# A two-layer block replanned: phi of the keys on GpSimd, query weights turned by DMA, MLP blocks of four tiles, last product in halves

## The chip, the core and the metric

The kernel runs on one core of one Trainium2 chip. The metric is the device time of one execution in microseconds (us). The engines are PE (TensorE, with PEld for its weight loads), DVE (VectorE), ACT (ScalarE), POOL (GpSimd) and SP, which here only issues DMAs. All runs quoted carry the state "fast".

## The reference, cut to what matters

The input has 2048 tokens (16 tiles of 128) of width 512, in bf16. Attention, then MLP, each with a residual; then both once more with the same weights.

```python
x = x + A(layernorm(x)); x = x + B(layernorm(x)); x = x + A(layernorm(x)); x = x + B(layernorm(x))

def A(x):                      # linear attention, 32 heads of 16
    q, k, v = heads(x @ wqkv)
    pq, pk = q @ w_phi, k @ w_phi
    phi_q = concat(softmax(pq), softmax(-pq)); phi_k = concat(softmax(pk), softmax(-pk))
    kv, z = phi_k^T @ v, sum(phi_k)          # over all 2048 tokens
    return ((phi_q @ kv) / (phi_q . z + 1e-6)) @ wo

def B(x):                      # gated MLP, inner width 1376
    return (relu(x @ W_gate) * (x @ W_up)) @ W_down
```

The sum over all tokens matters: no tile can be attended before the last tile's keys have been summed. From the start to that point ("the key phase") each tile is normalized and turned, multiplied by key and value weights, pushed through exp, divided by its row sums ("phi") and summed into `kv`. The query and key weights are first multiplied by `w_phi` ("the fold"), for which they have to be turned.

## The kernel before

The kernel writes all operations down with costs and priorities, lets a small planner of its own simulate them, and then issues them in the planned order. The order on each engine is thereby fixed; semaphores do the rest. The planner knows that some DVE instructions and POOL exclude each other (`port`).

```python
POOL_PHI = (1930, 1940)        # ns: occupies, latency
XPOSE = (1200, 2430)           # a DMA transpose
RATE = 265.0                   # bytes per ns for loads

def plan(ops):
    # ...
    for o in cand:
        t = max(clock[e], o.ready, port if o.port else 0.0, lanes[0] if o.move else 0.0)
    # ... the earliest goes next
    if o.port:
        port = t + occ
```

A tile's normalization in layer A runs on DVE and takes the port; so does phi on either engine:

```python
n = op("DVE", SCALE, due, lambda: nc.vector.tensor_scalar(
    out=xn.t[:], in0=x_of(t), scalar1=mv[:, t, 0:1], scalar2=rs[:, t:t + 1], op0=Alu.subtract,
    op1=Alu.mult), [a], [xn], name="xnA", port=True)
# ... in Keys.tile, after exp (ek), row sums (sk) and their reciprocals:
if phi_eng == "POOL":
    a = [op("POOL", POOL_PHI, due, lambda: phi(nc.gpsimd, 0, 2), [a], [ph], [ek, sk], name="phi", port=True)]
# ...
else:   # "BOTH": half on DVE, half on POOL; before, all 16 tiles of the first layer
    a = [op("DVE", dve(512), due, lambda: phi(nc.vector, 0, 1), [a], [ph], [ek, sk], name="phi", port=True),
         op("POOL", (965, 975), due, lambda: phi(nc.gpsimd, 1, 1), [a], (), [ek, sk, ph], name="phi", port=True)]
```

The MLP works on blocks of one or two tiles:

```python
BLOCKS = ((1, 1, 2, 2, 2, 2, 2, 2, 2), (1, 1, 2, 2, 2, 2, 2, 2, 1, 1))
# ... in mlp(l, t0, n, ...), with W = n * P columns:
for q, (g, m) in enumerate(fs):
    for b in range(NB):
        nc.tensor.matmul(ps.t[:m, q * W:(q + 1) * W], lhsT=w[:, b, g * P:g * P + m],
                         rhs=xT.t[:, b, 0:W], start=(b == 0), stop=(b == NB - 1))
```

The softmax here doesn't subtract the row's maximum and nothing guards it: scores larger than these inputs give would overflow.

Of the kernel before, what the change touches and what calls it, by code (L numbers as in the profile page):

```python
# [8 lines left out]
P = 128  # L9
# [227 lines left out]
XPOSE = (1200, 2430)  # L237
RATE = 265.0
# [16 lines left out]
BLOCKS = ((1, 1, 2, 2, 2, 2, 2, 2, 2), (1, 1, 2, 2, 2, 2, 2, 2, 1, 1))  # L255
# [3 lines left out]
def kernel(  # L259
# [25 lines left out]
    wk, wv, wq, wo = (new(n, [NB, D]) for n in ("wk", "wv", "wq", "wo"))  # L285
# [15 lines left out]
    p_wT = pool("wT", 1, [NB, D])  # L301
# [7 lines left out]
    p_xB = pool("xnTB", 3, [NB, 2 * P], fifo=True)  # L309
    p_h = pool("hT", 2, [NF * 2 * P], fifo=True)  # L310
# [15 lines left out]
    wqkv = A_wqkv.rearrange("(b p) f -> p b f", p=P)  # L326
    x_in = [None] * T
    x_in[0] = load(0, X[0][:, 0, :], xv[:, 0, :], 131072)
    l_wk = [load(0, wk[:, b:b + 2, :], wqkv[:, b:b + 2, D:2 * D], 262144, "ACT") for b in (0, 2)]
    l_wf = load(1, wf[:], A_w_phi.rearrange("(b j) d f -> (j d) b f", b=NB, j=8), 65536)  # L330
    x_in[1] = load(2, X[0][:, 1, :], xv[:, 1, :], 131072)
    l_wv = load(3, wv[:], wqkv[:, :, 2 * D:3 * D], 524288, "ACT")
    op("ACT", (1300, 1300), 5, lambda: nc.scalar.preload_act_table_set("natural_log_exp_and_others"), name="tbl")
    wov = A_wo.rearrange("(h bb c) f -> c h bb f", bb=NB, c=C)
    gv, uv = (w.rearrange("(b p) f -> p b f", p=P) for w in (B_W_gate, B_W_up))
    dv = B_W_down[0:10 * P, :].rearrange("(f p) d -> p f d", p=P)
    l_wq, l_wo, l_wg, l_wu, l_wd = [], [], [], [], []
    late = [("q", wq[:, b, :], wqkv[:, b, 0:D], 131072) for b in range(NB)]
    late += [("g", wg[:, b, :], gv[:, b, :], 352256) for b in range(NB)]
    late += [("o", wo[i * H:(i + 1) * H, :, :], wov[i], 131072) for i in range(C)]  # L340
    late += [("u", wu[:, b, :], uv[:, b, :], 352256) for b in range(NB)]
    late += [("d", wd[:, f:f + 2, :], dv[:, f:f + 2, :], 262144) for f in range(0, 10, 2)]
    late += [("d", wd[:96, 10, :], B_W_down[10 * P:F, :], 98304)]
    homes = dict(q=l_wq, g=l_wg, o=l_wo, u=l_wu, d=l_wd)

    def load_next(after, due):
        if late:
            kind, dst, src, nbytes = late.pop(0)
            homes[kind].append(load(due, dst, src, nbytes, follow=[after]))
# [29 lines left out]
    def fold(w, dst, loaded, due, step, engs):  # L379
        wT = Buf(p_wT)  # L380
        turned, done = [], []
        for m in range(NB):
            ps = Buf(p_b)
# [6 lines left out]
        for m in range(NB):  # L390
# [3 lines left out]
                start=True, stop=True) for b in range(NB)], [turned[m], c_blk] + turned[:m], [ps], [wT], name="fold")  # L394
# [7 lines left out]
    def turn(src, dst, how, due, after, takes, uses, name):  # L402
        if how == "SP":
            return op("SP", XPOSE, due, lambda: nc.sync.dma_start_transpose(out=dst(), in_=src.t[:]), [after],
                      takes, [src] + uses, name=name, move=500)
# [13 lines left out]
    def norm_A(l, t, due, after, how):  # L419
# [11 lines left out]
        return turn(xn, lambda: xnTA[c][:, :, i * P:(i + 1) * P], how, due, n, [], [], "xnTA")  # L431


    class Keys:
# [6 lines left out]
        def tile(self, t, due, due_v, due_z, xT, phi_eng, v_eng="ACT"):  # L441
# [12 lines left out]
                for b in range(NB)], [xT, l_wv], [vp], name="V")  # L454
# [119 lines left out]
    def mlp(l, t0, n, due_x, due_g, due_d, after, how):  # L574
# [3 lines left out]
        turned = []  # L578
        for i in range(n):
            t = t0 + i  # L580
            a = stats(l, "B", t, due_x(i), [after[t]])
            xc = Buf(p_xn)
# [6 lines left out]
            out=tmp[:, t0:t0 + n], in0=mv[:, t0:t0 + n, 1], scalar1=EPS, scalar2=None, op0=Alu.add), [a], name="ve")  # L589
# [44 lines left out]
        for i in range(n):  # L634
            t = t0 + i
            yp = Buf(p_b)
            last = None
            for lo, hi in ((0, 4), (4, 8), (8, NF)):
# [18 lines left out]
    for t in range(T):  # L657
        if t == 2:
            x_in[2] = load(4, X[0][:, 2, :], xv[:, 2, :], 131072)
            x_in[3] = load(5, X[0][:, 3, :], xv[:, 3, :], 131072)  # L660
# [86 lines left out]
```

## Time and profile before

| | before |
|---|---|
| median of the first 3 runs | 402.99 us |
| span of the profiled execution | 401.2 us |
| PE busy | 387.8 us (97%) |
| DVE, ACT, POOL busy | 275.5, 259.5, 22.1 us |

The top of the page and the engines' line, before. Busy PE is not PE at its peak: the record of a matmul of 512 columns is 0.379 us long, but the next one can start 0.216 us after it.

```profile
span 401.2 us, 8365 instructions
PE 387.8 (97%) x3176; PEld 265.9 (66%) x3176; DVE 275.5 (69%) x685; ACT 259.5 (65%) x704; POOL 22.1 (6%) x24
```

The table of stretches, before. Columns: the stretch in us, its length, then busy us (and instructions) of each engine, granted clock, share of DMA engines, GB/s.

```profile
core 0: us, PE busy (x) PEld busy (x) DVE busy (x) ACT busy (x) POOL busy (x), PEclk, DMA share, GB/s
10.00:40.00 30.00, 26.06 (x188) 14.02 (x188) 29.81 (x58) 25.20 (x78) 9.01 (x8) 1.00 0.60 138
40.00:62.00 22.00, 21.72 (x154) 12.09 (x155) 19.54 (x30) 20.63 (x59) 9.44 (x9) 1.00 0.62 174
62.00:80.00 18.00, 16.69 (x171) 11.38 (x170) 15.08 (x52) 18.00 (x60) 0.00 (x0) 1.00 0.13 23
80.00:250.00 170.00, 169.72 (x1326) 117.07 (x1324) 121.07 (x276) 106.69 (x283) 2.99 (x2) 1.00 0.16 31
```

From 80 to 250 us PE is full. From 10 to 40 us DVE is full (29.81 of 30) and PE is not. From 62 to 80 us ACT is full: the first attended tiles wait for one another's results there.

The chain of waits, before: start, length, what.

```profile
36.10 4.13 DMA xnTA<-xn
...
137.49 9.61 PE b L607 x88
...
397.08 0.75 DVE X L648
397.83 0.66 DVEq L742
```

88 gate and up matmuls of 256 columns take 9.61 us, 0.109 us each. A transposed tile took 4.13 us to land at 36.1 us. The kernel ends with a residual of 0.75 us on DVE and a store.

Phi and the normalizations of the first layer, before, from the views of these two tiles; the three durations are min/median/max in ns.

```profile
L466 POOL TENSOR_TENSOR phiK<-ek,sk x16: 1054/1056/1717, 16.5 to 58.9; 128x512 bf16<-128x512 bf16 x16
L466 DVE TENSOR_TENSOR phiK<-ek,sk x16: 652/692/1358, 17.9 to 58.8; 128x512 bf16<-128x512 bf16 x16
...
L427 DVE TENSOR_SCALAR xn<-X,mvA,rsA x16: 390/403/1097, 8.7 to 45.8; 128x512 bf16<-128x512 bf16 x16
```

### The profile page before, as it was taken

The page shows a single profiled execution, that of the slowest core. Times are in us where ns is not written, and L with a number is a line of the kernel's source. Part 1 is how long each engine was busy: PE and PEld are TensorE (multiplying, and loading weights), DVE is VectorE, ACT ScalarE, POOL GpSimd, SP SyncE. Part 2 cuts the span into 40 slices and gives each one's busy share as a digit, 9 for nine tenths or more (in the row PEclk, how much of TensorE's full clock was granted, in tenths as well). Part 3 has the DMA queues.
Part 4 walks back from the last instruction along what each step waited for, and adds up shares of the span by engine and source line. Part 5 has one row for each costly group of instructions (what it writes and reads, how often), then busy time and mean ns, then how long its engine had stood idle before and what let it go on. Part 6 is the DMA issues. An engine that isn't in the chain of part 4 may idle for free.

```text
span 401.2 us, 8365 instructions
## 1 busy us (share of the span) xinstructions
PE 387.8 (97%) x3176; PEld 265.9 (66%) x3176; DVE 275.5 (69%) x685; ACT 259.5 (65%) x704; POOL 22.1 (6%) x24
## 2 busy tenths in 40 slices
PE   6889999899999999999999999999999999999996
PEld 3454565667787678556777845576778686785784
DVE  6999896999995835787365457799998523132222
ACT  4888999977665355838464759997846353452542
POOL 0142350000000000000000002000000000000000
PEclk9999999999999999999999999999999999999999
DMA  6287940233331013101010100025333102001000
GB/s 211 63 192 159 262 118 0 42 67 63 71 68 41 0 28 67 26 15 28 2 26 2 28 0 2 1 41 81 68 65 68 28 26 68 13 29 39 15 28 28
DMA packets 54536, 21.83 MB, mean 54 GB/s; under 512 B 45952, under 2 KB 53472, under 8 KB 54496
## 3 DMA queue, kind: packets, MB, share of 16 engines
q1 hardware_dynamic: 53424, 20.25, 22.4%
q10 hardware_dynamic: 1072, 1.05, 0.8%
q8 instruction: 25, 0.41, 0.4%
q14 instruction: 15, 0.12, 0.1%
HBM read 8.44 MB, written 2.10 MB: 26 GB/s over the span
## 4 chain that ended last, share of the span: by engine, by line
PE 76%; DVE 14%; DMA 4%; ACT 3%; issue 2%; DVEq 0%; ACTq 0%
PE b L607 35%; PE b L642 18%; PE b L452 5%; PE b L446 5%; PE b L565 4%; PE b L518 3%; PE q L481 3%; DMA xnTA<-xn 3%; DVE pr L558 2%; ACT Eq L522 1%; DVE bstA L416 1%; PE q L536 1%; DVE X L569 1%; DVE m L553 1%; DVE o L561 1%
## 5 line engine op out<-in xcount | busy, mean ns | idle before, releaser
L619 ACT ACTIVATE gu<-b 128x512 bf16<-128x512 f32 (+1 forms) x102 | 55.5, 555 | 61.0 <-PE b L607 60.1
L607 PE MATMUL b<-xnTB,wg 128*128 128x256 bf16 (+3 forms) x836 | 92.9, 256 | 0.4 <-ACT Eq L522 0.3
L607 PE MATMUL b<-xnTB,wu 128*128 128x256 bf16 (+3 forms) x836 | 92.9, 256 | 0.2 <-ACT Eq L522 0.2
L625 DVE TENSOR_TENSOR hT<-gu 128x512 bf16<-128x512 bf16 (+1 forms) x102 | 38.5, 380 | 69.2 <-ACT gu L622 69.0
L642 PE MATMUL b<-wd,hT 128*128 128x512 bf16 (+1 forms) x352 | 82.8, 379 | 0.0
L607 PEld LDWEIGHTS <-wg 128*128 128x128 bf16 (+1 forms) x836 | 72.5, 100 | 11.4 <-issue 0.6
L607 PEld LDWEIGHTS <-wu 128*128 128x128 bf16 (+1 forms) x836 | 72.4, 100 | 8.1 <-issue 0.3
L622 ACT CAST gu<-b 128x512 bf16<-128x512 f32 (+1 forms) x102 | 54.8, 543 | 24.7 <-PE b L607 23.4
L642 PEld LDWEIGHTS <-hT 128*128 128x128 bf16 (+1 forms) x352 | 33.8, 98 | 34.8
L543 ACT CAST N<-q 128x384 bf16<-128x384 f32 (+1 forms) x96 | 48.1, 583 | 0.0
L522 ACT ACTIVATE Eq<-b 128x512 bf16<-128x512 f32 x64 | 40.4, 690 | 5.7 <-PE b L518 5.7
L457 DVE TENSOR_REDUCE sk<-ek 128x64 f32<-128x1024 bf16 x32 | 38.6, 1211 | 6.8 <-ACT ek L449 6.7
L648 DVE SCALAR_TENSOR_TENSOR X<-b,rsB,X 128x512 bf16<-128x512 f32 x32 | 23.3, 745 | 27.5 <-PE b L642 27.4
L449 ACT ACTIVATE ek<-b 128x512 bf16<-128x512 f32 x64 | 35.7, 603 | 8.9 <-PE b L446 8.6
L446 PE MATMUL b<-Wk,xnTA 128*128 128x512 bf16 x128 | 32.3, 380 | 4.2 <-DMA xnTA<-xn 2.1
L466 POOL TENSOR_TENSOR phiK<-ek,sk 128x512 bf16<-128x512 bf16 x18 | 21.4, 1193 | 226.6 <-ACT sk L462 221.9
L565 PE MATMUL b<-wo,oT 128*128 128x512 bf16 x128 | 32.5, 379 | 1.1 <-DVE X L569 0.4
L466 DVE TENSOR_TENSOR phiK<-ek,sk 128x512 bf16<-128x512 bf16 (+1 forms) x32 | 31.2, 977 | 2.4 <-ACT sk L462 2.3
L452 PE MATMUL b<-wv,xnTA 128*128 128x512 bf16 x128 | 32.2, 379 | 0.0
L518 PE MATMUL b<-xnTA,Wq 128*128 128x512 bf16 x128 | 31.7, 379 | 0.0
L543 ACT COPY DS<-q 128x48 f32<-128x48 f32 (+1 forms) x96 | 23.7, 318 | 7.2 <-PE q L536 6.1
L536 PE MATMUL q<-R,Eq 128*128 128x144 bf16 x256 | 25.1, 226 | 0.5 <-ACT N L543 0.4
(65 smaller groups left out, 376.1 us busy)
## 6 DMA issues: line engine op xcount, KB each, us to landing
out_dram<-X SPq DMA_DIRECT2D x16, 128.0 KB, 1.7
X<-in_A_x_dram SPq DMA_DIRECT2D x6, 256.0 KB, 4.0
wg<-in_B_W_gate_dram SPq DMA_DIRECT2D x4, 344.0 KB, 3.8
wu<-in_B_W_up_dram SPq DMA_DIRECT2D x4, 344.0 KB, 3.8
wd<-in_B_W_down_dram SPq DMA_DIRECT2D x5, 256.0 KB, 3.1
wk<-in_A_wqkv_dram ACTq DMA_DIRECT2D x2, 256.0 KB, 3.6
X<-in_A_x_dram SPq DMA_DIRECT2D x4, 128.0 KB, 4.4
wv<-in_A_wqkv_dram ACTq DMA_DIRECT2D x1, 512.0 KB, 5.4
```

What stands on the lines that cost most here:

```text
L446: k = op("PE", mm(4, 512), due, lambda: [nc.tensor.matmul(kp.t[:], lhsT=xnTA[c][:, b, cols], rhs=Wk2[:, b, :], start=(b == 0), stop=(b == ...
L452: v = op("PE", mm(4, 512), due_v, lambda: [nc.tensor.matmul(vp.t[:], lhsT=xnTA[c][:, b, cols], rhs=wv[:, b, :], start=(b == 0), stop=(b == ...
L457: a = op("DVE", SUM16, due, lambda: nc.vector.tensor_reduce(out=sk.t[:], in_=ek.t[:].rearrange("p s (h f) -> p (s h) f", f=DH), axis=AX.X, ...
L466: e.tensor_tensor(out=ph.t[:, s:s + n].rearrange("p s (h f) -> p (s h) f", f=DH), in0=ek.t[:, s:s + n].rearrange("p s (h f) -> p (s h) f", ...
L518: q = op("PE", mm(4, 512), due(c, b), lambda b=b, qp=qp: [nc.tensor.matmul(qp.t[:], lhsT=Wq2[:, m, b * P:(b + 1) * P], rhs=xnTA[c][:, m, : ...
L522: done.append(op("ACT", act(512), due(c, b), lambda b=b, s=s, qp=qp: nc.scalar.activation(out=Eq[c][:, b, s, :], in_=qp.t[:], func=AF.Exp, ...
L543: nc.scalar.copy(out=q[:, k, 0:3] if k < 2 else q[:, :, 3], in_=ps.t[:, 0:n * GE].rearrange("p (n c j) -> p n c j", n=n, j=HB)[:, :, lo:hi])
L565: a = op("PE", mm(4, 512), due + 3, lambda: [nc.tensor.matmul(yp.t[:], lhsT=oT.t[:, b, :], rhs=wo[:, b, :], start=(b == 0), stop=(b == NB ...
L607: nc.tensor.matmul(ps.t[:m, q * W:(q + 1) * W], lhsT=w[:, b, g * P:g * P + m], rhs=xT.t[:, b, 0:W], start=(b == 0), stop=(b == NB - 1))
L619: nc.scalar.activation(out=gu.t[:m, 0, lo * W:hi * W], in_=gp.t[:m, lo * W:hi * W], func=AF.Relu)
L622: nc.scalar.copy(out=gu.t[:m, 1, lo * W:hi * W], in_=up.t[:m, lo * W:hi * W])
L642: nc.tensor.matmul(yp.t[:], lhsT=h.t[:m, f * W + i * P:f * W + (i + 1) * P], rhs=wd[:m, f, :], start=(f == 0), stop=(f == NF - 1))
```

## The change

Its intent is to relieve DVE in the key phase (phi on POOL), to make loads and transposes fit each other (loads in another order and more thinly, a lower load rate and a longer transpose in the planner), to save PE work (query weights turned by DMA, blocks of four tiles) and to shorten the end. The diff, cut to its core:

```diff
-XPOSE = (1200, 2430)
-RATE = 265.0
+XPOSE, XPOSE_LOADS = (1200, 3600), (1200, 3600)
+RATE = 250.0
-BLOCKS = ((1, 1, 2, 2, 2, 2, 2, 2, 2), (1, 1, 2, 2, 2, 2, 2, 2, 1, 1))
+PHI = ["POOL"] * 15 + ["BOTH"]
+BLOCKS = ((1, 1, 2, 4, 4, 2, 2), (1, 1, 2, 4, 4, 2, 1, 1))
 ...
+    load_x(0, 1, 0)
+    l_wv = [load(0, wv[:, b:b + 2, :], ...) for b in (0, 2)]        # value weights first
+    load_x(1, 1, 1)
+    l_wk = [load(1, wk[:, b:b + 2, :], ...) for b in (0, 2)]
 ...
+            if by_dma:                                              # in fold(), for wq only
+                turned.append(op("SP", XPOSE_LOADS, due + m, lambda m=m: nc.sync.dma_start_transpose(
+                    out=wT.t[:, :, m * P:(m + 1) * P], in_=w[m * P:(m + 1) * P, :]), ...))
+                continue
 ...
+            halves = ((0, 256), (256, 512)) if l == 1 and t == T - 1 else ((0, 512),)   # last product
 ...
-            load_next(xT[t], ...); load_next(xT[t], ...)            # two weight loads per tile
+            load_next(xT[t], p["K0"] + p["KS"] * t)                 # one
-        keys.tile(t, k0, k0 + p["V0"], k0 + p["Z0"], xT[t], "BOTH")
+        keys.tile(t, k0, k0 + p["V0"], k0 + p["Z0"], xT[t], PHI[t])
```

More of the change, by code (lines that the diff above doesn't have):

```diff
@@ L283, in x_of @@
         return X[t // C][:, t % C, :]
-    wk, wv, wq, wo = (new(n, [NB, D]) for n in ("wk", "wv", "wq", "wo"))
+    wv, wo = new("wv", [NB, D]), new("wo", [NB, D])
     Wk2, Wq2 = new("Wk2", [NB, D]), new("Wq2", [NB, D])
@@ L300 @@
     p_a = p_b
-    p_wT = pool("wT", 1, [NB, D])
     p_xn = pool("xn", 4, [D])
@@ L308 @@
     p_o, p_oT = pool("o", 3, [D]), pool("oT", 4, [NB, P])
-    p_xB = pool("xnTB", 3, [NB, 2 * P], fifo=True)
-    p_h = pool("hT", 2, [NF * 2 * P], fifo=True)
+    p_xB = pool("xnTB", 2, [NB, 4 * P], fifo=True)
+    p_h = pool("hT", 2, [NF * 4 * P], fifo=True)
+    wk, wT_ = (p_h.tiles[i][:, lo:lo + NB * D].rearrange("p (b f) -> p b f", b=NB)
+                   for i, lo in ((0, 512), (1, 0)))
+    p_wT = Pool([wT_])
     p_gu = pool("gu", 3, [2, 512])
@@ L326, with load_x @@
     wqkv = A_wqkv.rearrange("(b p) f -> p b f", p=P)
+    def load_x(t, n, due, follow=()):
+        o = load(due, X[t // C][:, t % C:t % C + n, :], xv[:, t:t + n, :], n * 131072, follow=follow)
+        x_in[t:t + n] = [o] * n
     x_in = [None] * T
-    x_in[0] = load(0, X[0][:, 0, :], xv[:, 0, :], 131072)
-    l_wk = [load(0, wk[:, b:b + 2, :], wqkv[:, b:b + 2, D:2 * D], 262144, "ACT") for b in (0, 2)]
-    l_wf = load(1, wf[:], A_w_phi.rearrange("(b j) d f -> (j d) b f", b=NB, j=8), 65536)
-    x_in[1] = load(2, X[0][:, 1, :], xv[:, 1, :], 131072)
-    l_wv = load(3, wv[:], wqkv[:, :, 2 * D:3 * D], 524288, "ACT")
+    load_x(0, 1, 0)
+    l_wv = [load(0, wv[:, b:b + 2, :], wqkv[:, b:b + 2, 2 * D:3 * D], 262144, "ACT") for b in (0, 2)]
+    load_x(1, 1, 1)
+    l_wk = [load(1, wk[:, b:b + 2, :], wqkv[:, b:b + 2, D:2 * D], 262144, "ACT") for b in (0, 2)]
+    l_wf = load(2, wf[:], A_w_phi.rearrange("(b j) d f -> (j d) b f", b=NB, j=8), 65536)
     op("ACT", (1300, 1300), 5, lambda: nc.scalar.preload_act_table_set("natural_log_exp_and_others"), name="tbl")
+    for t in (2, 3):
+        load_x(t, 1, 3 + t)
+    for t in (4, 6):
+        load_x(t, 2, 3 + t)
     wov = A_wo.rearrange("(h bb c) f -> c h bb f", bb=NB, c=C)
@@ L336 @@
     dv = B_W_down[0:10 * P, :].rearrange("(f p) d -> p f d", p=P)
-    l_wq, l_wo, l_wg, l_wu, l_wd = [], [], [], [], []
-    late = [("q", wq[:, b, :], wqkv[:, b, 0:D], 131072) for b in range(NB)]
-    late += [("g", wg[:, b, :], gv[:, b, :], 352256) for b in range(NB)]
-    late += [("o", wo[i * H:(i + 1) * H, :, :], wov[i], 131072) for i in range(C)]
-    late += [("u", wu[:, b, :], uv[:, b, :], 352256) for b in range(NB)]
-    late += [("d", wd[:, f:f + 2, :], dv[:, f:f + 2, :], 262144) for f in range(0, 10, 2)]
-    late += [("d", wd[:96, 10, :], B_W_down[10 * P:F, :], 98304)]
-    homes = dict(q=l_wq, g=l_wg, o=l_wo, u=l_wu, d=l_wd)
+    l_wo, l_wg, l_wu, l_wd = [], [], [], []
+    late = [(l_wg, wg[:, b, :], gv[:, b, :], 352256) for b in range(NB)]
+    late += [(l_wu, wu[:, b, :], uv[:, b, :], 352256) for b in range(NB)]
+    late += [(l_wo, wo[i * H:(i + 1) * H, :, :], wov[i], 131072) for i in range(C)]
+    late += [(l_wd, wd[:, f:f + 2, :], dv[:, f:f + 2, :], 262144) for f in range(0, 10, 2)]
+    late += [(l_wd, wd[:96, 10, :], B_W_down[10 * P:F, :], 98304)]
     def load_next(after, due):
-        if late:
-            kind, dst, src, nbytes = late.pop(0)
-            homes[kind].append(load(due, dst, src, nbytes, follow=[after]))
+        home, dst, src, nbytes = late.pop(0)
+        home.append(load(due, dst, src, nbytes, follow=[after]))
     c_id = op("POOL", (900, 900), 0, lambda: make_identity(nc, ident[:]), name="ident")
@@ L377, in evac, with fold @@
         return op(eng, act(cols) if eng == "ACT" else dve(cols), due, copy, deps, takes, uses, name=name)
-    def fold(w, dst, loaded, due, step, engs):
+    def fold(w, dst, loaded, due, step, engs, by_dma=False):
         wT = Buf(p_wT)
@@ L382, in fold @@
         for m in range(NB):
+            if by_dma:
+                turned.append(op("SP", XPOSE_LOADS, due + m, lambda m=m: nc.sync.dma_start_transpose(
+                    out=wT.t[:, :, m * P:(m + 1) * P], in_=w[m * P:(m + 1) * P, :]), [loaded], [] if m else [wT],
+                    [wT] if m else [], name="wT", move=500))
+                continue
             ps = Buf(p_b)
@@ L393, in fold @@
                 ps.t[:, b * P:(b + 1) * P], lhsT=wT.t[:, b, m * P:(m + 1) * P], rhs=Wblk[:, b, :],
-                start=True, stop=True) for b in range(NB)], [turned[m], c_blk] + turned[:m], [ps], [wT], name="fold")
+                start=True, stop=True) for b in range(NB)], [turned[m], c_blk], [ps], [wT], name="fold")
             done.append(evac(engs[m % 2], due + step + m, lambda m=m: dst[:, m, :], lambda ps=ps: ps.t[:], [f], (),
@@ L399, with turn @@
     k_fold = fold(wk, Wk2, l_wk, 100, 100, ("ACT", "DVE"))
-    def turn(src, dst, how, due, after, takes, uses, name):
+    def turn(src, dst, how, due, after, takes, uses, name, cost=XPOSE):
         if how == "SP":
-            return op("SP", XPOSE, due, lambda: nc.sync.dma_start_transpose(out=dst(), in_=src.t[:]), [after],
+            return op("SP", cost, due, lambda: nc.sync.dma_start_transpose(out=dst(), in_=src.t[:]), [after],
                       takes, [src] + uses, name=name, move=500)
@@ L430, in norm_A @@
         c, i = t // C, t % C
-        return turn(xn, lambda: xnTA[c][:, :, i * P:(i + 1) * P], how, due, n, [], [], "xnTA")
+        return turn(xn, lambda: xnTA[c][:, :, i * P:(i + 1) * P], how, due, n, [], [], "xnTA",
+                    XPOSE if l else XPOSE_LOADS)
     class Keys:
@@ L453, in tile @@
                 vp.t[:], lhsT=xnTA[c][:, b, cols], rhs=wv[:, b, :], start=(b == 0), stop=(b == NB - 1))
-                for b in range(NB)], [xT, l_wv], [vp], name="V")
+                for b in range(NB)], [xT] + l_wv, [vp], name="V")
             v = evac(v_eng, due_v, lambda: vx.t[:, :, 0:P], lambda: vp.t[:].rearrange("p (b e) -> p b e", e=P),
@@ L577, in mlp @@
         W = n * P
-        turned = []
+        turned, seen = [], []
         for i in range(n):
@@ L581, in mlp @@
             a = stats(l, "B", t, due_x(i), [after[t]])
+            seen.append(a)
             xc = Buf(p_xn)
@@ L588, in mlp @@
         r = op("DVE", DVE0, due_g(0), lambda: nc.vector.tensor_scalar(
-            out=tmp[:, t0:t0 + n], in0=mv[:, t0:t0 + n, 1], scalar1=EPS, scalar2=None, op0=Alu.add), [a], name="ve")
+            out=tmp[:, t0:t0 + n], in0=mv[:, t0:t0 + n, 1], scalar1=EPS, scalar2=None, op0=Alu.add), seen, name="ve")
         r = op("DVE", DVE0, due_g(0), lambda: nc.vector.reciprocal(
@@ L635, in mlp, with down @@
             t = t0 + i
-            yp = Buf(p_b)
-            last = None
-            for lo, hi in ((0, 4), (4, 8), (8, NF)):
-                def down(yp=yp, i=i, lo=lo, hi=hi):
-                    for f in range(lo, hi):
-                        m = min(P, F - f * P)
-                        nc.tensor.matmul(yp.t[:], lhsT=h.t[:m, f * W + i * P:f * W + (i + 1) * P],
-                                         rhs=wd[:m, f, :], start=(f == 0), stop=(f == NF - 1))
-                last = op("PE", mm(hi - lo, 512), due_d(i) + lo, down,
-                          [made[f] for f in range(lo, hi)] + l_wd + ([last] if lo else []),
-                          [] if lo else [yp], [yp, h] if lo else [h], name="down")
-            x = x_of(t)
-            done.append(op("DVE", dve(512, 1, 130), due_d(i), lambda x=x, yp=yp, t=t: nc.vector.scalar_tensor_tensor(
-                out=x, in0=yp.t[:], scalar=rs[:, t:t + 1], in1=x, op0=Alu.mult, op1=Alu.add), [last, r], (), [yp],
-                name="resB"))
+            halves = ((0, 256), (256, 512)) if l == 1 and t == T - 1 else ((0, 512),)
+            for c0, c1 in halves:
+                yp, last = Buf(p_b), None
+                for lo, hi in ((0, 4), (4, 8), (8, NF)):
+                    def down(yp=yp, i=i, lo=lo, hi=hi, c0=c0, c1=c1):
+                        for f in range(lo, hi):
+                            m = min(P, F - f * P)
+                            nc.tensor.matmul(yp.t[:, 0:c1 - c0], lhsT=h.t[:m, f * W + i * P:f * W + (i + 1) * P],
+                                             rhs=wd[:m, f, c0:c1], start=(f == 0), stop=(f == NF - 1))
+                    last = op("PE", mm(hi - lo, c1 - c0), due_d(i) + lo + c0, down,
+                              [made[f] for f in range(lo, hi)] + l_wd + ([last] if lo else []),
+                              [] if lo else [yp], [yp, h] if lo else [h], name="down")
+                x = x_of(t)[:, c0:c1]
+                done.append((t, c0, c1, op("DVE", dve(c1 - c0, 1, 130), due_d(i), lambda x=x, yp=yp, t=t, w=c1 - c0:
+                             nc.vector.scalar_tensor_tensor(
+                                 out=x, in0=yp.t[:, 0:w], scalar=rs[:, t:t + 1], in1=x, op0=Alu.mult, op1=Alu.add),
+                             [last, r], (), [yp], name="resB")))
         return done
@@ L657 @@
     for t in range(T):
-        if t == 2:
-            x_in[2] = load(4, X[0][:, 2, :], xv[:, 2, :], 131072)
-            x_in[3] = load(5, X[0][:, 3, :], xv[:, 3, :], 131072)
-        if t >= 4 and t % 2 == 0:
-            x_in[t] = x_in[t + 1] = load(
-                p["K0"] + p["KS"] * (t - 5), X[t // C][:, t % C:t % C + 2, :], xv[:, t:t + 2, :], 262144,
-                follow=[xT[t - 4]] if t > 6 else [])
         xT.append(norm_A(0, t, p["K0"] - 4000 + p["KS"] * t, [x_in[t]], ("ACT", "DVE")[t % 2] if t < 4 else "SP"))
-        if t >= 3:
-            load_next(xT[t], p["K0"] + p["KS"] * t)
+        if t >= 4:
+            if t % 2 == 0 and t + 4 < T:
+                load_x(t + 4, 2, p["K0"] + p["KS"] * t, [xT[t]])
             load_next(xT[t], p["K0"] + p["KS"] * t)
         k0 = p["K0"] + p["KS"] * t
-        keys.tile(t, k0, k0 + p["V0"], k0 + p["Z0"], xT[t], "BOTH")
+        keys.tile(t, k0, k0 + p["V0"], k0 + p["Z0"], xT[t], PHI[t])
     while late:
         load_next(xT[-1], p["K0"] + p["KS"] * T)
-    q_fold = fold(wq, Wq2, l_wq, p["QF"], 100, ("ACT", "DVE"))
+    q_fold = fold(A_wqkv[:, 0:D], Wq2, k_fold[-1], 5000, p["QF"] - 5000, ("ACT", "DVE"), True)
     eq_free = [[] for _ in range(C)]
@@ L699 @@
                        "ACT" if t0 < 2 else "SP")
-            for i, a in enumerate(done):
-                t = t0 + i
+            for t, c0, c1, a in done:
+                i = t - t0
                 if l == 0:
@@ L707 @@
                 else:
-                    op("SP", (460, 1700), e0, lambda t=t: nc.sync.dma_start(
-                        out=ov[:, t, :], in_=x_of(t)), [a], name="store",
-                       move=131072 / RATE)
+                    op("SP", (460, 1700), e0, lambda t=t, c0=c0, c1=c1: nc.sync.dma_start(
+                        out=ov[:, t, c0:c1], in_=x_of(t)[:, c0:c1]), [a], name="store",
+                       move=256 * (c1 - c0) / RATE)
         xT = nxt
```

## The prediction

> **What bounds it now.** PE. The page shows PE busy 387.8 of 401.2 us, clock 1.0. Busy can hide waiting, so I count what PE had to stream: in the chain of waits four 128x512 matmuls take 0.86 us (0.216 each), 88 of 128x256 take 9.61 us (0.109 each). By that measure 80-250 us and 270-397 us are full. Not full: 0-10 us (6 us idle, plus 3.6 us of warm-up matmuls), 10-40 (5 us lost), 70-80 (2), 250-270 (2), and the 4 us after the final matmul (0.75 us residual on DVE, then the store). So 15 to 20 us can be had at all, 5 of them waiting for first loads.
>
> **The first 60 us** are held by DVE (table of stretches: 9.9 to 10.0 of each 10 us up to 40, 8.9 to 9.5 after) with ACT close behind (8.0 to 9.6). DVE spends 12.6 us there on its half of phi (16 x 789 ns). The chain also has two 4.13 us transposes of normalized tiles, at 18.8 and 36.1 us, against the usual 2.4 to 2.5; loads ran beside them.
>
> **What the change does, costed.**
> 1. phi of 15 first-layer tiles goes whole to POOL: DVE loses 11.8 us; POOL gains 15 halves of 1.06 us. The Trainium skill, "SBUF — State Buffer", section on who interferes with whom, says POOL and two-port DVE instructions exclude each other for a whole instruction; the trace agrees (one normalization took 1.10 instead of 0.40 us while POOL ran). With 2.1 us POOL instructions normalizations will wait longer. ACT becomes the next limit: it idles only about 6 us from 10 to 60.
> 2. wq turned by DMA: 16 PE matmuls (0.9 us) and four evacuations (2 x 0.68 DVE, 2 x 0.59 ACT) go; four transposes of 1.2 us issue come.
> 3. Value weights first: V(0) can start near 6.5 us, where the first K was at 10.2; the fold of wk runs beside it: 1.5 to 2 us.
> 4. Thinner loads, transposes planned at 3.6 us: fewer waits for transposes, 1 to 2 us (PE and its loads now wait 5.8 us for them, by that tile's view).
> 5. Four-tile blocks: 88 matmuls of 512 (19.03 us) for 176 of 256 (19.22): four times 0.19 = 0.8 us, all on the critical path.
> 6. Halved last product: the last residual shrinks from 0.75 to about 0.45 us, the last store is half: 0.3 to 0.5 us.
>
> Items 1 to 4 overlap: together I take 4 us out of the first 80, limited by ACT. With 0.8 + 0.4 that is about 5 us.
>
> **Predicted: 398 us**, range 394.5 to 401.5. Chances: faster by over 2% 0.12, within 2% 0.86, slower 0.02.
>
> **What would show it.** Last first-layer Q (61-65 us now) about 4 us earlier; DVE's share from 10 to 60 down to about 0.8, ACT's 0.93 or more; POOL busy 30 to 36 us; first V near 6.5 us, before K; transposes landing in 2.4 to 3.6 us; from 100 us on PE as full as before, G and Up together 0.8 us cheaper; the tail after the last matmul under 3.8 us.
>
> **What would make it wrong.** Normalizations stuck behind POOL, so DVE stays the limit; a DMA transpose from DRAM that delays x loads or first transposes; a four-tile block waiting for its fourth attention tile between 80 and 120 us, where DVE is full; or a schedule that also fills 70-80 and 250-270, giving 8 us or more.

## The result

| | before | changed |
|---|---|---|
| median | 402.53 us (6 runs) | 400.58 us (6 runs, 399.36 to 400.88) |
| ratio of mean times, with 95% interval | | 0.9943 (0.9919 to 0.9966) |
| span of the profiled execution | 401.2 us | 397.6 us |

A ratio is the mean time of one kernel's fast runs over that of the other's of the same rounds, so it isn't quite the ratio of the medians quoted. The changed kernel computes the right result and is faster by 0.6%, which is inside 2%.

The two profiled executions both had the full clock but flatter the change: 3.6 us apart, where the medians are 2 us apart. The profiled run of before was among the slower of its full-clock runs (402.96 us; the group reaches from 402.0 to 403.7), that of the changed kernel among the faster of its twelve. The page, changed kernel:

```profile
span 397.6 us, 7614 instructions
PE 384.3 (97%) x2819; PEld 231.8 (58%) x2819; DVE 268.1 (67%) x657; ACT 259.5 (65%) x694; POOL 33.6 (8%) x24
```

The table of stretches, changed kernel:

```profile
10.00:40.00 30.00, 28.97 (x194) 15.31 (x193) 29.20 (x55) 28.61 (x92) 17.42 (x10) 1.00 0.66 163
40.00:62.00 22.00, 19.87 (x149) 11.27 (x148) 14.94 (x16) 17.62 (x45) 12.96 (x7) 1.00 0.59 139
62.00:80.00 18.00, 15.70 (x182) 11.63 (x180) 16.44 (x55) 17.97 (x62) 0.00 (x0) 1.00 0.12 23
80.00:250.00 170.00, 170.00 (x1140) 99.96 (x1138) 118.71 (x272) 108.22 (x277) 2.57 (x2) 1.00 0.16 31
```

Read the PE column: 2.9 us more busy time from 10 to 40 us, then 1.85 us less from 40 to 62 and 1.0 less from 62 to 80. An early lead was won and mostly given back; the next section counts it.

The chain, changed kernel:

```profile
121.45 18.99 PE b L622 x88
...
394.23 0.48 DVE X L665
394.71 0.39 DVEq L753
```

88 matmuls of 512 columns take 18.99 us and replace 176 of 256 at 2 x 9.61 = 19.22. The last residual fell from 0.75 to 0.48 us.

Phi and the normalizations, changed kernel:

```profile
L480 POOL TENSOR_TENSOR phiK<-ek,sk x16: 1504/1930/2007, 16.1 to 56.8; 128x1024 bf16<-128x1024 bf16 x15, 128x512 bf16<-128x512 bf16 x1
L480 DVE TENSOR_TENSOR phiK<-ek,sk x1: 2358/2358/2358, 55.1 to 55.1; 128x512 bf16<-128x512 bf16 x1
...
L440 DVE TENSOR_SCALAR xn<-X,mvA,rsA x16: 378/406/2023, 6.1 to 44.3; 128x512 bf16<-128x512 bf16 x16
```

The longest normalization took 2.02 us instead of 1.10, and the one half of phi left on DVE took 2.36 us instead of 0.69.

### Where the time went

Both of these traces have all their matmul records, so I count what PE had to stream: every matmul at the spacing from start to start that these traces show where matmuls of one width follow each other (0.2158 us for 512 columns, 0.1092 for 256, 0.0558 for 128, and in between by columns). Without the eight warm-up matmuls that is 377.95 us before and 376.20 us after. The time on the clock less the work of the matmuls ended by then is PE's *lost time* (counted when a matmul starts instead, an entry is up to 0.4 us smaller):

| lost by (us) | 10 | 20 | 30 | 40 | 50 | 60 | 70 | 80 | 250 | 270 | last matmul |
|---|---|---|---|---|---|---|---|---|---|---|---|
| before | 8.0 | 10.2 | 12.3 | 13.4 | 13.9 | 14.0 | 14.1 | 16.6 | 17.3 | 19.7 | 19.7 |
| changed | 7.6 | 9.3 | 9.5 | 9.5 | 11.1 | 12.3 | 14.3 | 15.4 | 15.7 | 18.3 | 18.3 |
| difference | 0.4 | 0.9 | 2.8 | 3.9 | 2.8 | 1.7 | -0.2 | 1.2 | 1.6 | 1.4 | 1.4 |

So the 3.6 us between the two spans are 1.75 us less work (0.89 for the query weights' transposes, 0.86 for the blocks, less what the halved product costs), 0.4 us less after the last matmul, and 1.4 us less lost time. At 40 us the changed kernel had 3.9 us in hand; by 62 us it had lost 2 of them. (At 70 us the difference is even negative because the idle stretch of the first attended tiles comes earlier: the first product with `kv` starts at 61.6 us instead of 63.5, the first gate product at 72.7 instead of 73.8.)

What happened at 38 us shows in the order of time, DVE and POOL alone, changed kernel (start, length, engine and instruction; runs of the same instruction are merged; in brackets the idle time before and what ended it):

```profile
37.79 4.29 DVE L440 TENSOR_SCALAR xn<-X,mvA,rsA 128x512 bf16<-128x512 bf16 x3
...
36.12 5.80 POOL L480 TENSOR_TENSOR phiK<-ek,sk 128x1024 bf16<-128x1024 bf16 x3 [0.24 <-ACT rsA L437]
```

Three normalizations that usually take 0.4 us each took 4.29 us, exactly while three phi instructions ran back to back on POOL. The planner had meant otherwise: it put all three normalizations into a gap between two POOL instructions, at 37.70, 38.01 and 38.33 us, with the next phi at 38.64. On the chip POOL started its next phi at 38.01, 0.6 us before its planned time and just before the record of the second normalization starts (38.12), held the port, and did so again before the third (39.95 against 40.06). Against the plan, DVE's normalizations and row sums were 0.1 to 0.8 us late before this place; the row sums after it were 3.1 to 3.4 us late, to the last one of the key phase.

This gives theory A: *the early lead is given back because normalizations wait for whole POOL instructions.* Rivals: B, the last key tiles are held by something else (late loads beside the transposes, or ACT, which is at 28.61 of 30 us from 10 to 40); C, not a rival but a second question, why runs of the same kernel fall into two groups 1.3 us apart.

### The profile page after: what moved, and what is told of

Read it like the earlier page. It is cut to its first block, busy times and chain, and to the rows that moved or that the text cites. A ratio compares the mean times of both kernels' runs of the same rounds, so it can differ in the third digit from the quotient of the medians.

```text
span 397.6 us, 7614 instructions
## 1 busy us (share of the span) xinstructions
PE 384.3 (97%) x2819; PEld 231.8 (58%) x2819; DVE 268.1 (67%) x657; ACT 259.5 (65%) x694; POOL 33.6 (8%) x24
## 4 chain that ended last, share of the span: by engine, by line
PE 78%; DVE 3%; ACT 2%; issue 0%; DVEq 0%; ACTq 0%
PE b L622 39%; PE b L658 19%; PE b L579 6%; PE b L460 3%; PE b L466 3%; PE q L550 3%; PE b L532 2%; PE q L495 2%; DVE pr L572 1%; ACT Eq L536 1%; ACT N L557 1%; DVE X L583 0%; DVE m L567 0%; DVE o L575 0%; PE b L420 0%
## 5 line engine op out<-in xcount | busy, mean ns | idle before, releaser
L634 ACT ACTIVATE gu<-b 128x512 bf16<-128x512 f32 (+2 forms) x98 | 55.1, 573 | 65.5 <-PE b L622 62.9
L622 PE MATMUL b<-xnTB,wg 128*128 128x128 bf16 (+2 forms) x660 | 91.8, 279 | 0.1
L622 PE MATMUL b<-xnTB,wu 128*128 128x128 bf16 (+2 forms) x660 | 91.8, 280 | 0.0
L640 DVE TENSOR_TENSOR hT<-gu 128x512 bf16<-128x512 bf16 (+2 forms) x98 | 38.1, 394 | 73.9 <-ACT gu L637 73.6
L658 PE MATMUL b<-wd,hT 128*128 128x512 bf16 (+2 forms) x363 | 82.3, 373 | 0.0
L637 ACT CAST gu<-b 128x512 bf16<-128x512 f32 (+2 forms) x98 | 54.3, 563 | 25.7 <-PE b L622 25.0
L622 PEld LDWEIGHTS <-wg 128*128 128x128 bf16 x660 | 55.3, 100 | 26.3 <-issue 0.3
L622 PEld LDWEIGHTS <-wu 128*128 128x128 bf16 x660 | 55.1, 100 | 23.7
L480 POOL TENSOR_TENSOR phiK<-ek,sk 128x1024 bf16<-128x1024 bf16 (+1 forms) x18 | 32.9, 1846 | 212.8 <-DVE phiK L480 184.9
L471 DVE TENSOR_REDUCE sk<-ek 128x64 f32<-128x1024 bf16 x32 | 38.4, 1210 | 8.1 <-ACT ek L463 8.0
L665 DVE SCALAR_TENSOR_TENSOR X<-b,rsB,X 128x512 bf16<-128x512 f32 (+1 forms) x33 | 23.4, 727 | 25.2 <-PE b L658 25.2
L550 PEld LDWEIGHTS <-Eq 128*128 128x128 bf16 x256 | 19.3, 98 | 10.2 <-issue 1.8
```

Source lines behind the costliest of these rows:

```text
L471: a = op("DVE", SUM16, due, lambda: nc.vector.tensor_reduce(out=sk.t[:], in_=ek.t[:].rearrange("p s (h f) -> p (s h) f", f=DH), axis=AX.X, ...
L550: pe.append(op("PE", mm(len(groups), GE), due, lambda ps=ps, groups=groups: [nc.tensor.matmul(ps.t[:, n * GE:(n + 1) * GE], lhsT=Eq[c][:, ...
L634: nc.scalar.activation(out=gu.t[:m, 0, lo * W:hi * W], in_=gp.t[:m, lo * W:hi * W], func=AF.Relu)
L637: nc.scalar.copy(out=gu.t[:m, 1, lo * W:hi * W], in_=up.t[:m, lo * W:hi * W])
L658: nc.tensor.matmul(yp.t[:, 0:c1 - c0], lhsT=h.t[:m, f * W + i * P:f * W + (i + 1) * P], rhs=wd[:m, f, c0:c1], start=(f == 0), stop=(f == N ...
```

## The experiments

Each was timed in five rounds against the kernel before. The means are of full-clock runs, with their number; "ratio" is over all fast runs, as defined above. The excess is what the 16 normalizations of the first layer took beyond 0.41 us each, from each run's trace. (Some times in the expectations of e1 and e4 are about 0.25 us later than in the profile's views, as 38.4 for 38.1 us; differences between them are not affected.)

| run | median | ratio (95% interval) | full clock: mean (runs of 6) | excess of normalizations |
|---|---|---|---|---|
| control (changed kernel) | 399.87 | 0.9924 (0.9893 to 0.9955) | 399.31 (3) | 4.9 us |
| e1 phi on POOL in halves | 398.70 | 0.9888 (0.9861 to 0.9914) | 398.08 (3) | 2.5 |
| e2 phi shared, as before | 403.19 | 0.9994 (0.9962 to 1.0025) | 401.88 (1) | 0.5 |
| e3 old blocks, replanned | 403.31 | 1.0010 (0.9983 to 1.0037) | 403.20 (4) | 9.3 |
| e4 fence | 397.15 | 0.9849 (0.9820 to 0.9878) | 397.23 (5) | 1.3 |
| e5 filling matmuls | 399.33 | 0.9902 (0.9877 to 0.9927) | 399.37 (6) | 4.8 |
| e6 nudged plan | 399.48 | 0.9926 (0.9886 to 0.9966) | 399.30 (4) | 4.0 |
| e7 old blocks, start kept | 400.91 | 0.9941 (0.9913 to 0.9969) | 400.26 (3) | 4.9 |
| e8 fence and filling | 397.41 | 0.9844 (0.9814 to 0.9874) | 397.35 (6) | 1.3 |
| e9 old rates, replanned | 402.58 | 0.9973 (0.9939 to 1.0008) | 401.51 (2) | 7.1 |
| e10 searched plan a | 396.95 | 0.9833 (0.9800 to 0.9866) | 396.99 (6) | 0.2 |
| e11 searched plan b | 397.13 | 0.9839 (0.9807 to 0.9871) | 397.15 (6) | 0.2 |

The kernel before, in the same three sets of rounds, had full-clock means of 402.44 (6 of 11 runs), 402.57 (7 of 11) and 402.70 us (7 of 11), and dipped-clock means of 404.40, 404.58 and 405.03. At full clock the change itself is therefore worth 402.44 - 399.31 = 3.1 us. The control was timed in the first set only, with e1 to e3; e4 to e7 and e8 to e11 are the other two sets, each on another chip. The 0.26 us between the three means of before is how far a comparison across sets can be trusted.

### The changed kernel again (control)

No edit.

> The changed kernel once more, as the control for the three runs beside it. Expected 399.4 to 400.9 us, two groups of spans (397.6 and 398.8 us) as in its six runs so far. If its profile falls in the other group, the lost time of PE up to 40 us should show where the 1.2 us between the groups comes from (theory: the moment early in the run at which TensorE gets its full clock, which was 4.2 us in the profile of the changed kernel and 6.2 us in that of the kernel before).

The times came in the two expected groups: three full-clock runs at 399.23 to 399.46 us, three dipped ones at 400.29, 400.59 and 402.25. Its profile fell in the dipped group. The table of stretches, control:

```profile
5.70:9.10 3.40, 1.63 (x26) 1.29 (x24) 2.97 (x7) 2.39 (x7) 0.00 (x0) 1.00 0.84 287
9.20:12.50 3.30, 3.30 (x16) 1.67 (x14) 2.57 (x5) 1.58 (x3) 0.00 (x0) 0.50 0.32 73
12.60:20.00 7.40, 6.55 (x46) 3.50 (x46) 7.10 (x15) 6.81 (x22) 2.59 (x2) 1.00 0.37 88
```

The clock had been full, halved for one stretch from 9.2 to 12.6 us and came back. In the stretch before, PE was busy 1.63 of 3.4 us. My expectation had put the difference at the moment of the first full clock; that part was wrong, it is a second half-clock stretch. It also shifted everything behind: the three 2.0 us normalizations are there again, 1.25 us later (39.4, 41.3 and 45.5 us).

### e1: phi on POOL in two halves

```diff
-                a = [op("POOL", POOL_PHI, due, lambda: phi(nc.gpsimd, 0, 2), ...)]
+                a = [op("POOL", POOL_PHI, due, lambda: (phi(nc.gpsimd, 0, 1), phi(nc.gpsimd, 1, 1)), ...)]
```

The planner isn't told, and the order on every other engine is identical, instruction for instruction.

> Only POOL's instruction for phi is cut in two halves of 512 columns; every engine keeps its order. Theory A (the early lead of 4 us over the kernel before is given back because DVE normalizations wait for whole 1.93 us POOL instructions, 1.6 us each at 38.4, 40.3 and 44.5 us): each of these waits falls to about 1 us or less, the last K/V sum ends 1.5 to 2.5 us earlier than 59.2 us, and the run is 1 to 2.5 us faster than the control. Theory B (loads beside the transposes, or ACT, hold the last key tiles): the waits get shorter but the last K/V sum ends within 0.5 us of before and the time stays within 0.5 us of the control.

The view of the normalized tile, e1:

```profile
L440 DVE TENSOR_SCALAR xn<-X,mvA,rsA x16: 379/406/1150, 6.1 to 42.8; 128x512 bf16<-128x512 bf16 x16
```

The longest normalization fell from 2.02 to 1.15 us, and the last K/V sum ended at 57.9 us against 59.2 in the full-clock profile of the changed kernel, 1.3 us earlier where 1.5 to 2.5 were expected. The run is 1.2 us faster at full clock. The wait of a normalization follows the length of one POOL instruction, and the time follows the wait: theory A holds, at or just below the lower end of what it expected.

### e2: phi shared between DVE and POOL again

```diff
-PHI = ["POOL"] * 15 + ["BOTH"]
+PHI = ["BOTH"] * 16
```

> The changed kernel with phi of the first layer shared between DVE and POOL as in the kernel before, planned anew. My prediction counted phi on POOL as 11.8 us of relief for DVE, part of 4 us: by that, this is 1.5 to 3 us slower than the control (402 to 403). Theory A, in its strong form (the POOL instructions cost as much in waits as they relieve): within 0.7 us of the control.

The median is 3.3 us slower than the control; five of six runs were dipped, so that at full clock only one run against three is left (401.88 against 399.31, 2.6 us). Normalizations waited for only 0.5 us in all, but DVE carried 14.2 us of phi again and the last K/V sum ended at 64.4 us. So this comparison puts moving phi to POOL at about 2.5 to 3 us of gain, in spite of the waits, and speaks against the strong form of theory A. But this kernel was planned anew, and e3 shows that a new plan by itself can cost 3 us, so the gain of phi alone is not shown.

### e3: blocks of two tiles, planned anew

```diff
-BLOCKS = ((1, 1, 2, 4, 4, 2, 2), (1, 1, 2, 4, 4, 2, 1, 1))
+BLOCKS = ((1, 1, 2, 2, 2, 2, 2, 2, 2), (1, 1, 2, 2, 2, 2, 2, 2, 1, 1))
```

> The changed kernel with MLP blocks of two tiles, planned anew. Counted from matmul durations (19.22 against 18.99 us per four tiles, four times) this is 0.8 to 0.9 us slower than the control. Rival: the blocks of four cost as much in waits or in granted clock as they save, and this is the same or faster. PE's total streaming work should be 377.0 to 377.1 us against 376.2.

It was 3.9 us slower at full clock, neither of the two. The trace shows why this doesn't measure the blocks. The view of the normalized tile, e3:

```profile
L440 DVE TENSOR_SCALAR xn<-X,mvA,rsA x16: 376/408/2077, 7.8 to 49.2; 128x512 bf16<-128x512 bf16 x16
```

Another MLP made the planner choose another order for the first 60 us, where there is no MLP, and in that order six normalizations ran into POOL (9.3 us in excess, 4.9 in the control). Its last K/V sum ended at 62.0 us against 59.2 in the changed kernel, both at full clock: 2.8 of the 3.9 us were lost before any MLP. (Whether the work rose as expected can't be read from this trace, which lacks some 40 matmul records.) The blocks had to be measured with the start held still, as e7 does.

### e4: a fence on POOL

```diff
+            def fenced():
+                if seen_xn:      # tiles normalized since the last fence, in planned order
+                    nc.gpsimd.tensor_copy(out=fence[:], in_=seen_xn[-1][:, 0:1])
+                    seen_xn.clear()
+                phi(nc.gpsimd, 0, 2)
             if phi_eng == "POOL":
-                a = [op("POOL", POOL_PHI, due, lambda: phi(nc.gpsimd, 0, 2), ...)]
+                a = [op("POOL", POOL_PHI, due, fenced, ...)]
```

Seven one-column copies make POOL wait for the normalizations that the plan has put ahead of it. The order on every engine stays as it was.

> Every engine keeps the order of the changed kernel; POOL alone gets, before seven of its phi instructions, a one-column copy that reads the newest normalized tile, so that it can't start phi before the normalizations that the plan put ahead of it. Theory A (a POOL instruction slipping 0.2 to 0.4 us ahead of its planned place locks two normalizations out for 1.6 us each, and all that follows is late): the 2.0 us normalizations at 38.4, 40.3 and 44.5 us fall to about 0.4 us, the last K/V sum of the first layer ends 2.5 to 3.5 us earlier than in the control (60.7 us in the control's profile), and the run is 1.5 to 3 us faster than the control (397 to 398.5). Theory B (something else holds the last key tiles): the waits go and the time stays within 0.7 us of the control.

DVE and POOL in order of time, e4 at the place of the trouble:

```profile
38.45 1.18 DVE L442 TENSOR_SCALAR xn<-X,mvA,rsA 128x512 bf16<-128x512 bf16 x3
39.55 1.21 DVE L474 TENSOR_REDUCE sk<-ek 128x64 f32<-128x1024 bf16 x1
...
39.77 0.19 POOL L489 COPY fence<-xn 128x1 bf16<-128x1 bf16 x1 [1.25 <-DVE xn L442]
39.90 3.82 POOL L483 TENSOR_TENSOR phiK<-ek,sk 128x1024 bf16<-128x1024 bf16 x2
```

The three normalizations took 1.18 us instead of 4.29. POOL waited 1.25 us for them, and nothing was lost by that. The last K/V sum ended at 57.5 us, 1.65 us earlier than in the full-clock profile of the changed kernel, the first gate product started at 71.0 instead of 72.7 us, and the run is 2.1 us faster at full clock. (I had expected the sum 2.5 to 3.5 us earlier, measured from the dipped control, whose trace has it at 60.4; it was 2.9 by that measure, of which the clock accounts for more than 1.) One normalization at 42.2 us still took 1.66 us: there the plan itself has POOL first. Theory A holds, because only the waits were taken away, and B falls as the main cause. A smaller part of B stays open: the transpose of the first of the three tiles, issued beside five large weight loads, landed after 6.1 us in the changed kernel and still after 5.1 us here, and no run moved those loads.

### e5: filling matmuls

```diff
+    def filler(n):
+        return [nc.tensor.matmul(wps.t[:], lhsT=p_h.tiles[0][:, 0:P], rhs=p_h.tiles[0][:, 0:512],
+                                 start=True, stop=True) for _ in range(n)]
# two after the last transpose of wk, five after the transposes of the first tile
```

> The changed kernel with seven idle matmuls of 512 columns between 5.9 and 8.4 us, where PE waits; all orders kept. Theory C (the two groups of times, 399.4 and 400.7, are runs without and with a second half-clock stretch of 3.4 us near 9 us, which follows a clock window in which PE was idle for more than half): all or nearly all runs show a granted clock of 0.998 or more, none near 0.995, and the median falls by 0.5 to 1 us. Rival: the groups come from something else, and both clocks still appear.

All six runs had the full clock and lay within 0.3 us (399.26 to 399.56). The table of stretches, e5:

```profile
5.70:9.10 3.40, 3.40 (x31) 2.26 (x29) 2.87 (x6) 2.30 (x7) 0.00 (x0) 1.00 0.87 297
9.20:12.50 3.30, 2.90 (x23) 1.52 (x22) 3.30 (x7) 2.49 (x5) 0.00 (x0) 1.00 0.28 64
```

These are the control's stretches, and here the second keeps its clock. But the clock of this trace rises at 7.20 us, so its own windows lie elsewhere, and the test is the count of runs: none of the 24 runs with filling matmuls (e5, e8, e10, e11) had the dipped clock, 27 of the 54 other runs of the changed kernel and its variants had it. The clock records of the traces say more: in each trace the clock changes at multiples of 3.41 us after its first rise. In the five traces with a half-clock stretch (control, e2, e6, e7, e9) PE was busy for 1.40 to 1.65 us of the 3.41 us before it; in no other such window of the 14 traces, up to the last matmul, was it busy for less than 1.74 us. So theory C holds, with its "idle for more than half". The mean at full clock did not move (399.37 against 399.31), so filling gains nothing but the dip. It takes away what makes some runs slow: the median fell by 0.5 us.

### e6: the plan nudged

```diff
-RATE = 250.0
+RATE = 251.0
```

> The changed kernel planned with an assumed load rate of 251 instead of 250 and otherwise the same: how much does a plan move the time when nothing real was changed? By the planner's own model this plan ends 1.4 us later. If the time moves by 1 us or more, single parts of the change that were planned anew (the shared phi, the old blocks) carry that much noise, and the title's load rate is a choice among plans rather than a cause. If it stays within 0.4 us, replanning is harmless and those results stand as they are.

The order changed, the planner's model said 1.4 us later, and at full clock nothing moved (399.30). But one run with a clock of 0.991 took 403.92 us, and in this order two normalizations waited 2.0 us again (4.0 us in excess in all). One nudge is one sample: together with e3 it says that a new plan may cost nothing or 3 us, and that the planner's model doesn't tell which: run again, it ends e3 and e6 both 1.45 us later than the changed kernel.

### e7: blocks of two tiles, the first 443 operations kept

```diff
+FIRST = [...]            # the changed kernel's first 443 operations, up to its first MLP block
+    return plan(ops, FIRST)
-BLOCKS = ((1, 1, 2, 4, 4, 2, 2), (1, 1, 2, 4, 4, 2, 1, 1))
+BLOCKS = ((1, 1, 2, 2, 2, 2, 2, 2, 2), (1, 1, 2, 2, 2, 2, 2, 2, 1, 1))
-    p_xB = pool("xnTB", 2, [NB, 4 * P], fifo=True)
+    p_xB = pool("xnTB", 3, [NB, 2 * P], fifo=True)
```

> MLP blocks of two tiles again (three buffers of two tiles for the turned input), but the first 443 operations, up to the first block at about 66 us, keep the order of the changed kernel. Theory: blocks of four save only the 0.8 us of streaming work, so this is 0.6 to 1.2 us slower than the control, and the first run with old blocks lost the other 2.5 us by its replanned first 60 us. Rival: blocks of four save more than their streaming work, and this is 2.5 us slower or more.

It is 0.95 us slower at full clock. Blocks of four are worth their streaming work and no more; the other 2.9 us of e3 came from its new plan, nearly all of it from the start, by the 2.8 us of its last K/V sum.

### e8: fence and filling matmuls

The edits of e4 and e5 together, orders as in the changed kernel.

> The fence and the seven filling matmuls together, all orders as in the changed kernel. If theories A and C are independent, their gains add: every run with a granted clock of 0.998 or more, and the time that the fence alone showed at full clock, 396.9 to 397.3 us, in every run. If the filling matmuls now delay something that the fence made critical, 397.5 or more.

All six runs had the full clock, at 397.02 to 397.72 us, mean 397.35; four of them were 0.1 to 0.4 us above the range expected. The fence alone already had five full-clock runs of six at 397.23, so that little was left for the filling to gain.

This trace has all its matmul records, so its lost time can be counted like that of the pair. With the seven filling matmuls counted as lost, it is 9.5 us at 40 us, as in the changed kernel, but 9.7 at 60 (changed: 12.3), 13.0 at 80 (15.4) and 15.8 at the last matmul (18.3). With the normalizations ahead of POOL, the lead that the changed kernel gave back is kept: this is the closest test of theory A.

### e9: the old load rate and transpose time in the planner

```diff
-XPOSE, XPOSE_LOADS = (1200, 3600), (1200, 3600)
-RATE = 250.0
+XPOSE, XPOSE_LOADS = (1200, 2430), (1200, 2430)
+RATE = 265.0
```

> The changed kernel planned with the old assumptions (transposes landing after 2.43 us always, 265 as the load rate), nothing else. My prediction gave thinner loads and longer planned transposes 1 to 2 us: by that 400.4 to 401.4 us at full clock against the control's 399.4. By the reading of the traces (waits for turned tiles are small in both kernels from 20 us on, the port decides) it depends on how many normalizations this plan happens to put behind POOL: time should follow the sum of their excess over 0.41 us, 4.8 us in the control, at about 0.5 us for each us.

It is 2.2 us slower at full clock, by two runs. Normalizations waited 7.1 us in excess, 2.3 more than in the control; at the half microsecond per microsecond that I had put down this explains about 1.1 us. The other half stays open, because this kernel was planned anew as a whole. The planner's own model, run again, ends this plan 2.15 us later than the changed kernel's, though it assumes faster loads and shorter transposes: it is a worse plan even by its own assumptions, so the run says little of what the loads and transposes themselves cost.

### e10 and e11: searched plans with fence and filling

From e8: random noise on the planner's priorities, a few other settings (among them 2.03 us instead of 1.93 for phi on POOL), many plans tried in the planner's model, two of the best taken. The fence now also stands before POOL's half of a shared phi.

```diff
+SEED, SIGMA = 100153, 100.0        # e11: 100773, 100.0
 # in refine(), after each backward pass:
+        for o in ops:
+            o.due += rng.gauss(0, SIGMA)
-PHI = ["POOL"] * 15 + ["BOTH"]
+PHI = (["POOL"] * 4 + ["BOTH"]) * 3 + ["BOTH"]      # e11: ["POOL"] * 14 + ["BOTH"] * 2
```

> Fence and filling matmuls, with the best plan of a search over starting priorities (planned 1.3 us shorter than the changed kernel's plan; phi shared on every fifth tile). With the fence the port keeps the planned order, so the plan should be kept: 395.3 to 396.5 us, faster than fence and fill. If gains of 1 us in the plan are below what the model knows, 396.5 to 398.

> As the run before, with another plan of the search (planned 0.9 us shorter than the changed kernel's plan; phi shared on the last two tiles). Expected 395.8 to 397 us; if gains of this size in the plan are below what the model knows, 396.5 to 398.

Normalizations waited 0.2 us in all, and all runs had the full clock. e10 is at 396.99 us, e11 at 397.15, both 0.2 to 0.4 us better than e8, where the planner had promised 0.9 to 1.3 us over the changed kernel's plan. e10 has the best median of all (396.95, 0.9833 of before, 1.7%; its interval reaches 2%, so whether it is faster by that much is unclear), but it can't be told apart from e4, e8 and e11: their intervals overlap. All four beat the changed kernel.

## Why the prediction was right or wrong

The 398 us and its range of 394.5 to 401.5 held the measured 400.58, and "within 2%" came out. The gain, 5 us by the sum, was 2.3 us by the ratio (0.0057 x 402.5) and 3.1 us at equal clock. The range, 1 to 8 us of gain, was wide enough to hold half the forecast gain. Point by point:

- **PE bounds the kernel, with about 15 to 20 us of slack at most: right.** Lost time up to the last matmul was 19.7 us before and is 18.3 us now.
- **"Together I take 4 us out of the first 80, limited by ACT": this is the step that was mis-sized.** The profiled pair shows 2.1 us by 80 us: 1.2 us less lost time and 0.9 us of work saved on the query weights. The lead did reach 3.9 us in lost time at 40 us. What took it back is what item 1 named ("normalizations will wait longer") and gave no number: 4.8 us of excess on normalizations and 1.7 us on DVE's one half of phi, against 0.7 and 1.7 before. With the fence the run is 2.1 us faster still, and e8 is 4.5 us ahead of before by 80 us (3.6 of lost time, 0.9 of work), so the 4 us were there. ACT is not what limited it: its share from 10 to 60 us was 0.89, not the predicted 0.93 or more, and it waited 2.8 us at one place for row sums of a blocked DVE. DVE's share was 0.87, not about 0.8. With the fence alone both come out as predicted, 0.93 and 0.81.
- **Item 1, phi on POOL: right in sign, as far as shown.** e2, which undoes it, is 2.6 us (one run at full clock) to 3.3 us (medians) slower, but it has a new plan, which may be part of that. POOL was busy 30 us from 10 to 60 us, as predicted (30 to 36).
- **Item 3, value weights first: wrong.** V(0) was predicted near 6.5 us and started at 9.28, though before the first K (10.37); lost time at 10 us fell by 0.4 to 0.9 us, depending on how matmuls in flight are counted, not by 1.5 to 2. The diff writes the value weights first, but the planner moved the key weights ahead. Issues and starts in order of time, changed kernel (`hT` is where `wk` now lies):

```profile
0.73 0.98 ACTq L326 DMA_DIRECT2D hT<-in_A_wqkv_dram  x2
1.74 2.42 ACTq L326 DMA_DIRECT2D wv<-in_A_wqkv_dram  x2
4.20 1.28 ACT L340 ACT_TABLE_LOAD   x1 [4.20 <-DMA hT<-in_A_wqkv_dram]
9.28 1.03 PE L466 MATMUL b<-wv,xnTA 128*128 128x512 bf16 x4
```

  The second half of `wv` was issued at 3.8 us and took 5.0 us to land, so V(0) could not start before 8.8 us; from 8.38 to 9.28 us PE ran the fold of `wk`, which stands before V(0) in its order. ACT, busy issuing until 4.2 us, loaded its table 1.9 us later than before. No run has the value weights really loaded first; what that would give stays open.
- **Item 4, thinner loads and longer planned transposes: not separable.** e9 comes near the predicted 1 to 2 us (2.2 by two runs), but it is planned anew, half of it goes with port waits, and its plan is longer by the planner's own count. One transposed tile took 6.1 us to land, more than the predicted 3.6; the median of the first layer's twelve was 3.1, against 3.0 before.
- **Item 2, query weights by DMA: the work fell by the predicted 0.9 us.** No run undid it alone.
- **Item 5, blocks of four: right.** Predicted 0.8 us; 0.86 counted, 0.95 measured by e7.
- **Item 6, the halved product: right in the profile.** From the end of the last matmul to the end of the span 3.5 us became 3.1. It was not run alone.
- **Last first-layer Q about 4 us earlier: nearly.** It ended at 65.4 instead of 68.9 us. (The "61-65 us now" in the prediction was a misreading of the trace.)
- **What the prediction didn't see at all: the two clocks.** 7 of the 12 runs of the changed kernel had the dipped clock, and that costs some 1.3 to 1.7 us by the group means (399.43 and 400.70 in the first six, 399.31 and 401.04 in the control). The kernel before has it too, at about 2 us, in 13 of 33 runs.

## What to carry to other kernels

A planned order holds on each engine, but not between two engines that exclude each other. Here both had work ready, POOL came 0.6 us before its planned time, and two normalizations of 0.4 us each took 2.0 us, the length of one POOL instruction each. Give the long one a true dependency on the short ones that the plan puts first, or cut it up; here one-column copies were worth 2.1 us. When a part of a scheduled kernel is to be measured, hold the rest of the order still, and compare runs at the same granted clock.

## What the Trainium skill lacked or had wrong

- "SBUF — State Buffer", section "Who interferes with whom": that the pair is held for a whole instruction and that the first to issue gets it agrees with the runs (normalizations of 0.41 us took 2.02 us behind a 1.93 us POOL instruction, 1.15 us behind one of 1.06). It doesn't say what happens with queues on both sides: the engines alternated, each of two normalizations waited for one whole POOL instruction of its own (2.02 and 2.01 us), so that three short ones took 4.29 us.
- The page doesn't say how to hold a planned order between computing instructions of the two engines. The runs show a one-column POOL copy that reads the DVE result first (0.19 us each, seven of them, 2.1 us of run time); halves on POOL shorten the wait (1.2 us of run time).
- "TensorE: Matmul & The Clock Gate", section "What's actually happening": the window of 3.4 us agrees (half clock in the control from 9.2 to 12.6 us). The table there has the clock fall after at least one idle window, and the section "Why this matters for your kernels" asks for no idle gaps over about 3 us. Here it fell after a stretch in which PE was busy 1.63 of 3.4 us, with no gap in it longer than 1.5 us. In the full-clock profile of the changed kernel PE was busy for only 1.30 us from 5.7 to 9.1 us and the clock stayed full, but that stretch is no window there: the page calls the window free-running, and this trace's clock rises at 4.20 us and falls at 396.73, 115 windows of 3.413 us apart, so that its window went from 4.20 to 7.61 us, with PE busy for 1.91 us. Over all 14 traces 1.40 to 1.65 us of busy PE in a window were followed by the half clock, 1.74 us or more were not.
- The same page calls the ramp a penalty of less than 1% that varies from run to run. The size agrees (1.3 to 1.7 us of 400), but here it was a second half-clock stretch after the ramp; the page lacks that this splits the runs of one kernel into two groups, which was as large as half the effect studied here, and that seven filling matmuls in the first gaps end it (399.26 to 399.56 us in all six runs).
